# Gate logits of six row blocks from three bf16 parts, put two units later

## The chip, the cores and the metric

One core of a Trainium2 chip runs the whole program. The metric is the device time of one execution in microseconds. Five engines work on it side by side, each with its own queue in program order: TensorE (PE, with its weight loads PEld), VectorE (DVE), ScalarE (ACT), GpSimd (POOL) and SyncE (SP), which issues most DMAs. POOL issues the indirect DMAs, the gathers and scatters by row numbers.

## What is computed

Attention in chunks, then two mixture-of-experts layers, all in float32. The second layer chooses one expert for a token from the first layer's output, so the first layer's rows have to be multiplied by the second layer's gate weights:

```python
def _moe_ref(x, w_gate, w_noise, noise, w1, w2):        # layer one, 1536 rows of 512, 8 experts
    noisy = x @ w_gate + np.log1p(np.exp(x @ w_noise)) * noise
    top2, top2_w = ...                                   # two experts for a row, with weights
    out[mask] += top2_w[mask, k, None] * (np.maximum(x[mask] @ w1[e], 0) @ w2[e])

def _moe2_ref(x, w_gate, w1, w2, capacity):              # layer two
    logits = x @ w_gate                                  # the gate logits
    expert_idx = np.argmax(logits, axis=1)
    ...
```

## The kernel before

Attention runs first (0 to about 75 us). Then come jobs, one for an expert and its rows, in the order `V0, V8, S0 to S6` (layer one) and `U0, UL, R0 to R6` (layer two). A job gathers its rows (POOL), turns them on PE (`x_block`) while the job before still runs, and works in **units**: in an M job (up to 384 rows) eight units of `layer1`, then two units of `rows` for each block of 128 rows. A W job (more rows, or V8) makes its second product in turned form. Products are made in three passes of fp32r parts (`mm3`), for which ACT rounds each raw weight tile (`whi`, L792) and DVE takes the rest (`wlo`, L793).

The finished rows of a block are scattered and added into the DRAM tensor `x_rows`, with the eight gate logits of layer two behind each row. Blocks of V0 and of the M jobs S4, S5 and S6 (ten in all) get their logits in two steps, which stand in the list `todo` and are taken one in a unit, after the unit's matmuls: `row_columns` turns the rows on PE and ACT copies them to `yt` (L1021, L1022); `row_logits` multiplies them by `wg2` in fp32 (L1028), DVE copies the eight columns behind the row (L1029), and POOL scatters (L1035), with a small memset ahead. The second step is called put here. Before, it followed one unit after the first.

After the matmuls of a unit comes what `due` gives: the turning of the next job's rows, hooks, and the splits of weight tiles. So a unit's ACT queue holds, in this order, the eviction of the unit, the copy to `yt`, the next job's `xh`, and `whi`.

During V8 the routing of layer one still runs on DVE between the units (one-hot products, L443 to L483). At the end of S4 `overflow_done` calls `rest1`, a loop for rows over an expert's place, which stands in a branch that is not taken with these inputs; every engine reads the count, passes the branch (L1273) and raises its semaphore behind it. In S6 the list of U0's rows is made from the logits of all jobs up to S5 (`early`), and U0's gather and first turning follow in S6's last units.

Of the kernel before, what the change touches and what calls it, by code (L numbers as in the profile page):

```python
# [8 lines left out]
F32 = mybir.dt.float32  # L9
F32R = mybir.dt.float32r  # L10
F16 = mybir.dt.float16
BF = mybir.dt.bfloat16
I32 = mybir.dt.int32
AF = mybir.ActivationFunctionType
OP = mybir.AluOpType
AX = mybir.AxisListType
# [42 lines left out]
def attention_two_moe_kernel(  # L59
# [7 lines left out]
    nc = tc.nc  # L67
    B, H, S, D = q.shape
    NM = mem_k.shape[2]
    DM, E = w_gate1.shape  # L70
    FF = w1a.shape[2]
# [5 lines left out]
    KD = DM // 128  # L77
# [5 lines left out]
    W2 = DM + 8  # L83
# [8 lines left out]
    pools = {}  # L92

    def pool(name, side="left", **kw):
        st_ = ExitStack()
        pools[name] = st_
        return st_.enter_context(tc.tile_pool(name=name, bufs=1, side=side, **kw))

    consts = pool("consts")
# [8 lines left out]
    def bank(tag):  # L108
        return ps["p"].tile([128, 512], F32, name="ps" + tag, bufs=2)
# [85 lines left out]
    xb, st = {}, {}  # L195
    lgs = axp.tile([128, NT, 2 * V], F32, name="lgs")
    noi = axp.tile([128, NT, V], F32, name="noi")
    wg1 = consts.tile([128, KD, 2 * V], F32, name="wg1")
    wg2 = consts.tile([128, KD, E], F32, name="wg2")

    def xs(t):
        if t not in xb:
            xb[t] = axp.tile([128, DM], F32, name="xs", bufs=4)
        return xb[t]
# [11 lines left out]
    act_copy = lambda d, s: nc.scalar.activation(d, s, AF.Copy)  # L216
# [180 lines left out]
    def y_consts():  # L397

        for i in range(2):
            nc.vector.tensor_copy(yid[:, :, i, 0:128], ident[:, None, :].to_broadcast([128, KD, 128]))  # L400
            nc.vector.tensor_copy(yid[:, :, i, 128:136], wg2)
        nc.vector.tensor_tensor(yid[:, :, 0, 136:144], wg2, yid[:, :, 0, 128:136], op=OP.subtract)
        nc.vector.tensor_copy(yid[:, :, 1, 136:144], zero[:, 0:32].rearrange("p (k e) -> p k e", k=KD))

    def all_of(gen):

# [394 lines left out]
    def x_block(xg, blk, C, tag="B", later=False):  # L801
        n = min(128, C - 128 * blk)
        p = bank(tag)
        pv = p.rearrange("p (k n) -> p k n", k=KD)
        for c in range(KD):
            nc.tensor.transpose(pv[:, c, 0:128], xg[:, c * 128:(c + 1) * 128], ident)  # L806
        o = slice(128 * blk, 128 * blk + n)
        xh, xl = st["x"]
        nc.scalar.activation(xh[:, :, o], pv[:, :, 0:n], AF.Copy)  # L809
        low = lambda: nc.vector.tensor_tensor(xl[:, :, o], pv[:, :, 0:n], xh[:, :, o], op=OP.subtract)  # L810
        if not later:
            low()
        return low
# [199 lines left out]
        nc.scalar.activation(yr[:n, 0:DM], ps[:n], AF.Copy, scale=g[:n])  # L1013
        return yr

    def row_columns(yr, n):

        p = bank("B")
        pv = p.rearrange("p (k n) -> p k n", k=KD)
        for k in range(KD):  # L1020
            nc.tensor.transpose(pv[:, k, 0:n], yr[:n, 128 * k:128 * k + 128], ident[:n, :n])  # L1021
        nc.scalar.activation(st["yt"][:, :, 0:n], pv[:, :, 0:n], AF.Copy)  # L1022

    def row_logits(yr, n):

        p = bank("D")
        for k in range(KD):
            nc.tensor.matmul(p[:n, 0:E], st["yt"][:, k, 0:n], wg2[:, k], start=k == 0, stop=k == KD - 1)  # L1028
        nc.vector.tensor_copy(yr[:n, DM:W2], p[:n, 0:E])  # L1029
# [56 lines left out]
    class Job:  # L1086


        def __init__(self, kind, n0, C, first, ids=None, gate=None, cols=None):
            self.kind, self.n0, self.C, self.first = kind, n0, C, first  # L1090
            self.nb = -(-C // 128)
            self.ids, self.gate, self.cols, self.oids = ids, gate, cols, None
            self.W = W1 if first else W2
            self.whole = C == 64 or cols == 0
            self.late = None
            self.turns = {"W": [8, 10, 12, 14], "M": [8, 9, 10, 11], "T": TT}[kind]
            self.xg = None
            self.later = []
            self.pops = 4 if kind == "T" else 1
            self.quiet = 0 if kind == "T" else 1  # L1100
            self.pool = ()
            self.weigh = 1 if kind == "T" else 5
            self.prev = []
            self.g = []

        def fetch(self):
# [28 lines left out]
        def rows(self, blk, half_, between=None):  # L1135
            if self.cols == 0:
                rows0(half_, between)
            else:
                rows2(self.n0, blk, half_, self.C, between)
            if half_ == 0:  # L1140
                return
            n = min(128, self.C - 128 * blk)
            yr = weighted(st["l2"], self.g[blk], n)
            if self.first:
                def put():
                    row_logits(yr, n)
                    scatter(yr, n, self.ids[blk], True, self.prev)
                self.todo += [lambda: row_columns(yr, n), put]
                return
            f = lambda: scatter(yr, n, (self.oids or self.ids)[blk], False, self.prev)  # L1150
            if self.oids is None:
                self.later.append(f)
            else:
                f()
# [113 lines left out]
    def rest1(wa, wb, ov, en, nb, after):  # L1268

        fl, idf, nvi = ov  # L1270
        n = nc.values_load(nvi[0:1, 0:1], min_val=0, max_val=V * nb)
        b_ = wp["C"]
        with tc.If(n > 0):  # L1273
            with tc.For_i(0, n):
                se, _, idi = picked(b_, fl, idf, nb)
                r = expert_of(b_, se, en)
                xg = b_.tile([128, 4, 256], F32, name="oraw", bufs=1).rearrange("p k f -> p (k f)")
                gather(x_d, idi[:, 0:1], xg[:, 0:W1])
                x_block(xg, 0, 128)
                g = wp["A"].tile([128, 1], F32, name="gs", bufs=10)  # L1280
                gate1(xg, se, g)
                hi, lo = st["y"]

                def part(src):

                    raw = b_.tile([128, 4, 256], F32, name="oraw", bufs=1)
                    nc.sync.dma_start(raw, src)
                    nc.scalar.activation(hi[:, :, 0:256], raw, AF.Copy)
                    nc.vector.tensor_tensor(lo[:, :, 0:256], raw, hi[:, :, 0:256], op=OP.subtract)
                    return [(hi[:, k, 0:256], lo[:, k, 0:256]) for k in range(4)]  # L1290

                xh, xl = st["x"]
                for f in range(4):
                    ws = part(wa[ds(r, 1)].rearrange("e (k p) f -> p (e k) f", p=128)[:, :, 256 * f:256 * f + 256])
                    ps = bank("A")
                    mm3(ps[:, 0:256], [((xh[:, k, 0:128], xl[:, k, 0:128]), ws[k]) for k in range(KD)])
                    nc.scalar.activation(st["hr"][:, 256 * f:256 * f + 256], ps[:, 0:256], AF.Relu)
                for c in range(2):
                    turn(c, 128)
                hh, hl = st["h"]  # L1300
                ps = bank("C")
                for c in range(2):
                    for j in range(2):
                        ws = part(wb[ds(r, 1)].rearrange("e (k p) f -> p (e k) f", p=128)
                                  [:, 4 * j:4 * j + 4, 256 * c:256 * c + 256])
                        mm3(ps[:, 256 * c:256 * c + 256],
                            [((hh[:, 4 * j + k, 0:128], hl[:, 4 * j + k, 0:128]), ws[k]) for k in range(4)],
                            j == 0, j == 1)
                yr = weighted(ps, g, 128)
                row_columns(yr, 128)  # L1310
                row_logits(yr, 128)
                scatter(yr, 128, idi[:, 0:1], True, [])
            after()
# [122 lines left out]
    V0 = Job("T", 0, caps1[0], True, cols=0)  # L1436
# [4 lines left out]
    n = 0  # L1441
# [86 lines left out]
    wp["B"] = pool("wpB")  # L1528
    st["h"] = (wp["B"].tile([128, FB, CM], F32R, name="hh"), wp["B"].tile([128, FB, CM], F32R, name="hl"))
    st["hr"] = wp["B"].tile([128, FF], F32, name="hr")  # L1530
    st["yt"] = wp["B"].tile([128, KD, 128], F32, name="yt")
    st["hf"] = st["yt"].rearrange("p k (j n) -> p (k j) n", n=64)
    st["h0"] = wp["B"].tile([128, 4, 128], F32, name="h0"), st["yt"]
# [5 lines left out]
    S = [Job(kind1(caps1[1 + s]), 4 + 4 * s, caps1[1 + s], True) for s in range(E - 1)]  # L1539
# [80 lines left out]
    def drain():  # L1620
        if bg["gen"] is not None:
            all_of(bg["gen"])
            bg["gen"] = None
# [174 lines left out]
    def overflow_done():  # L1798

        drain()  # L1800

        rest1(w1a, w2a, ov[1], en1, NB1, lambda: x_block(S[5].xg[0], 0, S[5].C))

    hooks = {}
    bg["gen"], bg["next"] = chain(), bg["credit"]
# [37 lines left out]
    U0.late = drain  # L1843
    U0.weigh = UWE
    U0.pool = (1, 3)
    S[0].quiet = S[-1].quiet = U0.quiet = 0
    U0.turns = [2 * U0.nb + 6.5]
    S[-1].turns = [11, 12, 13]
# [10 lines left out]
    for job in jobs[1:-1]:  # L1859
        n = job.n0  # L1860
# [71 lines left out]
```

## Time and profile before

| | |
|---|---|
| time, median of 3 runs | 598.99 us (598.37 to 599.94) |
| the profiled execution | 599.92 us, span 598.1 us |
| PE busy | 582.7 us (97%), 4536 matmul passes |
| DVE, ACT, POOL busy | 62%, 51%, 28% |
| granted clock of PE | 0.999 of full speed |
| `wg2` product (L1028) | 80 passes, 10 blocks |

The page gives the busy time of each engine; the timeline gives single instructions with start and duration, and in brackets the idle time before them with what ended it. Passes of PE overlap, so what a group costs is read from start to start.

### The profile page before, as it was taken

The numbers are of one execution on the slowest core, as the hardware profiler recorded it, in microseconds if no ns is written. First come the engines' busy times: TensorE is split into PE (matmuls) and PEld (weight loads), VectorE is DVE, ScalarE is ACT, GpSimd is POOL, SyncE is SP. The second block draws the span as 40 slices with busy tenths as digits, with TensorE's granted clock in tenths as the row PEclk, the third lists the DMA queues.
The fourth block names the chain that finished last, engine by engine and source line by source line (L and its number), as shares of the span: only waits on it lengthen the run. The fifth ranks groups of instructions, "written<-read, shape, count | busy, mean of one in ns | idle before, by whom it ended". The sixth has DMA issues, their size and how long they took to land. (4 is left out here: it accounts for less than half of the span.)

```text
span 598.1 us, 12264 instructions
## 1 busy us (share of the span) xinstructions
PE 582.7 (97%) x4536; PEld 519.6 (87%) x4548; DVE 369.9 (62%) x984; ACT 303.7 (51%) x638; POOL 166.6 (28%) x242
## 2 busy tenths in 40 slices
PE   8999999999999999999999999999999999999996
PEld 5798756899999999999998898988978978879984
DVE  7888766977555556555555257273668648457672
ACT  5764543455445445445455345344427657466562
POOL 8896104135213114113130321202341121220110
PEclk9999999999999999999999999999999999999999
DMA  9996747475856757647455674654376586975750
GB/s 265 278 214 169 232 128 231 125 228 158 278 159 129 232 159 188 187 130 175 142 110 160 141 157 137 121 140 130 40 248 221 172 267 214 393 270 179 245 188 25
DMA packets 75293, 110.13 MB, mean 184 GB/s; under 512 B 28083, under 2 KB 28083, under 8 KB 75226
## 3 DMA queue, kind: packets, MB, share of 16 engines
q1 hardware_dynamic: 65866, 84.72, 45.5%
q0 software_dynamic: 9360, 24.54, 17.9%
q8 instruction: 38, 0.62, 0.4%
q14 instruction: 29, 0.24, 0.1%
HBM read 88.63 MB, written 20.48 MB: 182 GB/s over the span
## 5 line engine op out<-in xcount | busy, mean ns | idle before, releaser
L793 DVE TENSOR_TENSOR wlo<-raww,whi 128x512 fp32r<-128x512 f32 x226 | 150.4, 689 | 40.1 <-ACT whi L792 38.7
L792 ACT ACTIVATE whi<-raww 128x512 fp32r<-128x512 f32 x228 | 135.6, 624 | 4.3 <-PE psA L858 1.7
L870 DVE SCALAR_TENSOR_TENSOR hl<-psA,hh 128x256 fp32r<-128x256 f32 (+7 forms) x104 | 53.4, 513 | 74.7 <-ACT hh L869 71.0
L869 ACT ACTIVATE hh<-psA 128x256 fp32r<-128x256 f32 (+7 forms) x104 | 47.3, 455 | 99.0 <-PE psA L858 91.6
L858 PE MATMUL psA<-xh,wlo 128*128 128x256 f32 (+7 forms) x416 | 84.8, 325 | 1.5 <-issue 0.7
L858 PE MATMUL psA<-xl,whi 128*128 128x256 f32 (+7 forms) x416 | 82.3, 320 | 0.0
L858 PE MATMUL psA<-xh,whi 128*128 128x256 f32 (+7 forms) x416 | 82.1, 319 | 0.0
L1035 POOL DMA_INDIRECT x_rows<-yr,ids x25 | 39.2, 1570 | 124.3 <-ACT whi L792 82.0
L858 PEld LDWEIGHTS psA<-xh,wlo 128*128 128x128 f32 x416 | 66.4, 188 | 3.8 <-issue 1.2
L858 PEld LDWEIGHTS psA<-xl,whi 128*128 128x128 f32 x416 | 68.1, 188 | 0.7 <-DVEq L1273 0.2
L858 PEld LDWEIGHTS psA<-xh,whi 128*128 128x128 f32 x416 | 68.2, 188 | 0.3
L798 POOL DMA_INDIRECT xg<-x_rows,ids x37 | 37.8, 1022 | 109.9 <-DVE gs L1075 40.8
L858 PE MATMUL psC<-wlo,hh 128*128 128x512 f32 (+1 forms) x184 | 52.7, 406 | 0.0
L858 PE MATMUL psC<-whi,hh 128*128 128x512 f32 (+1 forms) x184 | 51.1, 396 | 0.0
L858 PE MATMUL psC<-whi,hl 128*128 128x512 f32 (+1 forms) x184 | 50.1, 394 | 0.0
L810 DVE TENSOR_TENSOR xl<-psB,xh 128x512 fp32r<-128x512 f32 (+4 forms) x32 | 20.4, 639 | 36.7 <-ACT xh L809 34.7
L858 PEld LDWEIGHTS psC<-whi,hl 128*128 128x128 f32 (+1 forms) x184 | 34.1, 186 | 8.2
L858 PEld LDWEIGHTS psC<-whi,hh 128*128 128x128 f32 (+1 forms) x184 | 33.9, 186 | 8.2
L858 PE MATMUL psA<-hh,wlo 128*128 128x312 f32 (+4 forms) x160 | 36.8, 351 | 0.8 <-DVE hl L870 0.5
L809 ACT ACTIVATE xh<-psB 128x512 fp32r<-128x512 f32 (+4 forms) x32 | 17.7, 555 | 38.8 <-PE psB L806 36.2
L858 PEld LDWEIGHTS psC<-wlo,hh 128*128 128x128 f32 (+1 forms) x184 | 32.1, 186 | 5.6
L1013 ACT ACTIVATE yr<-psC,gs 128x512 f32<-128x512 f32 (+1 forms) x24 | 16.5, 687 | 39.2 <-PE psC L858 34.9
(368 smaller groups left out, 922.2 us busy)
## 6 DMA issues: line engine op xcount, KB each, us to landing
raww<-in_moe_w_dram SPq DMA_DIRECT2D x114, 512.0 KB
raw<-in_k_dram SPq DMA_DIRECT2D x6, 512.0 KB
raw<-in_q_dram SPq DMA_DIRECT2D x6, 512.0 KB
x_rows<-xs SPq DMA_DIRECT2D x12, 256.0 KB
out_dram<-zero SPq DMA_DIRECT2D x3, 1024.0 KB
x_rows<-zero POOLq DMA_DIRECT2D x5, 520.0 KB
v<-in_v_dram SPq DMA_DIRECT2D x10, 256.0 KB
whi<-in_moe_w_dram SPq DMA_DIRECT2D x4, 512.0 KB
```

Source lines behind the costliest of these rows:

```text
L792: nc.scalar.activation(hi[:, c], raw, AF.Copy)
L793: (eng or nc.vector).tensor_tensor(lo[:, c], raw, hi[:, c], op=OP.subtract)
L798: return nc.gpsimd.indirect_dma_start(out=xg, out_offset=None, in_=src, in_offset=bass.IndirectOffsetOnAxis(ap=ids_ap, axis=0))
L809: nc.scalar.activation(xh[:, :, o], pv[:, :, 0:n], AF.Copy)
L810: low = lambda: nc.vector.tensor_tensor(xl[:, :, o], pv[:, :, 0:n], xh[:, :, o], op=OP.subtract)
L858: nc.tensor.matmul(ps, w[a], x[b], start=first and i == 0, stop=last and i == n - 1)
L869: nc.scalar.activation(hh[:, f, 0:C], ps[:, 0:C], AF.Relu)
L870: nc.vector.scalar_tensor_tensor(hl[:, f, 0:C], ps[:, 0:C], 0.0, hh[:, f, 0:C], op0=OP.max, op1=OP.subtract)
L1013: nc.scalar.activation(yr[:n, 0:DM], ps[:n], AF.Copy, scale=g[:n])
L1035: wr = nc.gpsimd.indirect_dma_start(out=x2_d, out_offset=off, in_=yr[:n], in_offset=None, compute_op=OP.add)
```

## The change

The gate weights `wg2` are split once, on POOL, into three bf16 parts (`wg3`, 24 columns). For one block of V0, two of S4, two of S5 and one of S6 the turned rows `yt` are split into three bf16 parts `y3`, in the memory of `hr`: first part by ACT, difference by POOL, second part by ACT, third part by POOL. Their logits are twelve bf16 matmuls of 24 columns instead of four fp32 matmuls of eight, and DVE adds the three groups of eight while it copies them out. The put of such a block now comes two units after the turning: if the job's next block is turned then, right before that, in the same step; otherwise behind two empty steps. The overflow loop gets its own tile for `hr`.

```diff
+    wg3 = consts.tile([128, KD, 3 * E], BF, name="wg3")
+    wgr = consts.tile([128, KD, E], F32, name="wgr")
...
+        three(nc.gpsimd.tensor_copy, [wg3[:, :, E * i:E * i + E] for i in range(3)], wg2, wgr)
+
+    def three(put, b, x, r):
+
+        put(b[0], x)
+        nc.gpsimd.tensor_tensor(r, x, b[0], op=OP.subtract)
+        put(b[1], r)
+        nc.gpsimd.tensor_tensor(b[2], r, b[1], op=OP.subtract)
...
-    def row_columns(yr, n):
+    def row_columns(yr, n, parts=False):
...
+        if parts:
+            three(act_copy, st["y3"], st["yt"], st["h0"][0])
-    def row_logits(yr, n):
+    def row_logits(yr, n, parts=False):
         p = bank("D")
+        if parts:
+            for k in range(KD):
+                for i in range(3):
+                    nc.tensor.matmul(p[:n, 0:3 * E], st["y3"][i][:, k, 0:n], wg3[:, k],
+                                     start=k + i == 0, stop=k == KD - 1 and i == 2)
+            nc.vector.tensor_reduce(yr[:n, DM:W2], p[:n, 0:3 * E].rearrange("p (s e) -> p e s", s=3),
+                                    axis=AX.X, op=OP.add)
+            return
...
             if self.first:
+                parts = n == 128 and blk < self.parts
                 def put():
-                    row_logits(yr, n)
+                    row_logits(yr, n, parts)
                     scatter(yr, n, self.ids[blk], True, self.prev)
-                self.todo += [lambda: row_columns(yr, n), put]
+                before, self.put = self.put, put
+
+                def columns():
+                    if before is not None:
+                        before()
+                    row_columns(yr, n, parts)
+                self.todo.append(columns)
+                if blk == self.nb - 1 or blk >= self.parts:
+                    self.todo += [lambda: None] * (2 if parts else 0) + [put]
+                    self.put = None
                 return
...
+    st["y3"] = [st["hr"].bitcast(BF)[:, 512 * i:512 * i + 512].rearrange("p (k n) -> p k n", k=KD) for i in range(3)]
...
+        op = pool("op", "right")
+        hr, st["hr"] = st["hr"], op.tile([128, FF], F32, name="ohr")
         rest1(w1a, w2a, ov[1], en1, NB1, lambda: x_block(S[5].xg[0], 0, S[5].C))
+        st["hr"] = hr
+        pools["op"].close()
...
+    for job, m in ((V0, 1), (S[4], 2), (S[5], 2), (S[6], 1)):
+        job.parts = m
```

## Rows read from the trace of the kernel before

**Rows 1.** The page, part 1: busy us (share of the span) xinstructions.
```profile
PE 582.7 (97%) x4536; PEld 519.6 (87%) x4548; DVE 369.9 (62%) x984; ACT 303.7 (51%) x638; POOL 166.6 (28%) x242
```

**Rows 2.** Timeline of PE in S5: start us, us, engine, line, operation, count.
```profile
369.18 1.09 PE L858 MATMUL psC<-whi,hl 128*128 128x512 f32 x4
370.11 0.95 PE L1028 MATMUL psD<-wg,yt 128*128 128x8 f32 x8
370.92 1.21 PE L858 MATMUL psC<-wlo,hh 128*128 128x512 f32 x4
```

**Rows 3.** Timeline of PE in U0's stage.
```profile
436.41 1.17 PE L858 MATMUL psC<-whi,hl 128*128 128x512 f32 x4
437.43 0.47 PE L496 MATMUL psD<-oh_Rl,oh_Ll 128*128 128x27 f16 x12
437.74 0.94 PE L858 MATMUL psC<-wlo,hh 128*128 128x512 f32 x3
```

**Rows 4.** Timeline of ACT in V8's stage.
```profile
103.95 0.60 ACT L1022 ACTIVATE yt<-psB 128x512 f32<-128x512 f32 x1
104.45 0.62 ACT L792 ACTIVATE whi<-whi 128x512 fp32r<-128x512 f32 x1
```

**Rows 5.** V8's stage: DVE's busy time in a window, timelines of DVE and PE.
```profile
104.00:118.50 14.50, 13.75 (x33) 1.00 0.51 144
...
105.10 0.69 DVE L793 TENSOR_TENSOR wlo<-whi 128x512 fp32r<-128x512 f32 x1
106.06 0.48 DVE L870 SCALAR_TENSOR_TENSOR hl<-psA,hh 128x312 fp32r<-128x312 f32 x1 [0.27 <-ACT hh L869]
...
116.45 0.84 PE L858 MATMUL psA<-hh,wlo 128*128 128x312 f32 x4 [0.50 <-DVE hl L870]
```

**Rows 6.** POOL by line (busy us, mean ns | idle); timelines of POOL and DVE.
```profile
L1035 POOL DMA_INDIRECT x_rows<-yr,ids x25 | 39.2, 1570 | 124.3 <-ACT whi L792 82.0 <-DVE wlo L793 18.1 <-issue 5.7
...
L793 POOL TENSOR_TENSOR wlo<-raww,whi 128x512 fp32r<-128x512 f32 x2 | 2.6, 1292 | 2.5 <-ACT whi L792 2.5
...
51.84 2.64 POOL L140 COPY v<-v 32x520 f32<-32x520 f32 x4
...
53.21 0.64 DVE L564 TENSOR_TENSOR nz<-nz,lgs 128x32 f32<-128x32 f32 x1
...
81.44 0.23 DVE L564 TENSOR_TENSOR nz<-nz,lgs 128x64 f32<-128x64 f32 x1
```

**Rows 7.** PE's waits at L858 (us, times); DVE's instruction at L1273 (first, last start).
```profile
  DVEq L1273: 0.2, 1
  ACTq L1273: 0.2, 1
...
L1273 DVEq EVENT_SEMAPHORE  x1: 21/21/21, 339.5 to 339.5; - x1
```

**Rows 8.** Timeline of PE in S4 and S5: the turning of later blocks.
```profile
334.42 0.60 PE L1021 MATMUL psB<-ident,yr 128*128 128x128 f32 x4
...
373.82 0.60 PE L1021 MATMUL psB<-ident,yr 128*128 128x128 f32 x4
...
380.02 0.60 PE L1021 MATMUL psB<-ident,yr 128*128 128x128 f32 x4
```

**Rows 9.** Timelines of DVE, POOL and ACT at the end of S4.
```profile
331.70 0.17 DVE L1029 COPY yr<-psD 128x8 f32<-128x8 f32 x1 [1.32 <-PE psD L1028]
...
332.60 1.76 POOL L1035 DMA_INDIRECT x_rows<-yr,ids  x1 [17.37 <-ACT whi L792]
...
335.12 0.60 ACT L1022 ACTIVATE yt<-psB 128x512 f32<-128x512 f32 x1 [2.43 <-PE psB L1021]
...
337.83 0.69 ACT L1013 ACTIVATE yr<-psC,gs 128x512 f32<-128x512 f32 x1 [1.59 <-PE psC L858]
```

**Rows 10.** Timelines of POOL and PE in S6: U0's gather and its turning.
```profile
405.18 1.02 POOL L798 DMA_INDIRECT xg<-x_rows,ids_u  x1 [18.96 <-DVE ids_u L1701]
...
410.04 0.66 PE L806 MATMUL psB<-ident,xg 128*128 128x128 f32 x4 [0.57 <-DMA xg<-x_rows,ids_u]
```

More of the change, by code (lines that the diff above doesn't have):

```diff
@@ L1103, in __init__ @@
             self.prev = []
+            self.parts = 0
+            self.put = None
             self.g = []
@@ L1144, in rows @@
             if self.first:
+                parts = n == 128 and blk < self.parts
                 def put():
-                    row_logits(yr, n)
+                    row_logits(yr, n, parts)
                     scatter(yr, n, self.ids[blk], True, self.prev)
-                self.todo += [lambda: row_columns(yr, n), put]
+                before, self.put = self.put, put
[6 more added lines that the diff above has]
+                    self.todo += [lambda: None] * (2 if parts else 0) + [put]
+                    self.put = None
                 return
```

## The prediction

> **What bounds the kernel now.** I read the page first: TensorE (PE) is busy for 97% of the span [rows 1], so a change pays only if it shortens PE's own line of work, and costs wherever it makes PE wait. Next I read how long a block's gate logits hold that line [rows 2], and what a run of short 16-bit matmuls costs in the same place [rows 3]. Then, since the new work lies on ScalarE (ACT) and GpSimd (POOL), the timelines of the stages where the six blocks stand: the first job of layer one (V8's stage, 104 to 119 us), the end of S4 (327 to 340), the end of S5 (373 to 380) and the end of S6 (405 to 410). In each I asked which engine ends the next wait of PE.
>
> In V8's stage it is not PE. VectorE (DVE) is busy for 13.75 of 14.50 us [rows 5], and PE waits for its `hl` [rows 5]. At the end of S4 every engine passes the branch of `rest1` (L1273); behind it PE's first matmul waits for ACT's event and its fifth for DVE's, 0.2 us each [rows 7]. At 410.04 PE waits 0.57 us for U0's gathered rows [rows 10]. From S4 to S6 there is otherwise no idle time of PE worth a row.
>
> **PE's part of the change.** The eight passes of the fp32 product hold PE from 370.11 to 370.92, 0.81 us, where a group of four matmuls takes 0.93 [rows 2]. Twelve f16 matmuls of 27 columns with twelve different weights hold it for 0.31 us [rows 3]; the new twelve (bf16, 24 columns) are of that form, so I take 0.31. That saves 0.50 a block, 3.0 us for six, if PE is the bound in every place. The reduction that replaces the copy on DVE reads 24 columns instead of eight; the copy takes 0.17 [rows 9], and three times that size on DVE cannot cost more than 0.1 more (an estimate). It sits in PE's shadow and counts as nothing; if that is gone it costs 0.6 in all.
>
> **The path of the three parts.** After the transposes ACT makes `yt` as before, then b0 (ACT), the rest r (POOL), b1 (ACT), the second rest b2 (POOL). An ACT copy of 128x512 takes 0.62 us and starts 0.50 after the one before it [rows 4]. A POOL subtraction of that size takes 1.29 us [rows 6]; there is no row with a bf16 operand, so this is the nearest, and the bounds are a one-input POOL copy of 520 columns (2.64/4 = 0.66 [rows 6]) and twice 1.29. I allow 0.07 us for each hand-over (an estimate). b1 stands in ACT's queue: from the end of b0 to the end of b1 (1.29 + 0.62 + 0.14 = 2.05 us) ACT does nothing for anyone. Behind it wait the weight splits `whi`, with them DVE's `wlo`, and the evictions `hh` and `yr`. That is the cost; "two units later" protects only PE's read of b2.
>
> *V0's block (in V8's stage).* Before, `whi` follows `yt` at 104.45 and `wlo` starts at 105.10 [rows 4, 5]. Now b0 takes that place and ends at 105.07, POOL is free and does r until 106.43, b1 ends at 107.12, `whi` at 107.64. Meanwhile b2 runs on POOL from 107.19 to 108.48. DVE operations with two SBUF inputs stretch beside a POOL operation that reads SBUF: the small L564 took 0.64 us beside the `v` copies, and with twice the elements 0.23 alone [rows 6]. `wlo` is such an operation, so I start it at 108.5, not 107.7: 3.4 (or 2.6) us late. DVE has 0.27 us of idle time before the next `hl` [rows 5], and the copy that moves away gives 0.1 back: 3.0 us remain (2.2 without the blocking). DVE works without a break until 119 and PE already waits for it, 0.50 us at 116.45 [rows 5], so they go through to PE one for one, and the 0.50 saved is swallowed there. **+3.0.**
>
> The Trainium skill ("SBUF — State Buffer", Who interferes with whom) states this as a rule: a DVE instruction with two SBUF inputs and a GpSimd instruction that reads SBUF exclude each other, and the one that issues second waits to the end. The stretched L564 agrees. By the rule the wait is the whole of b2, as taken; were it not so, V8's loss would be 2.2 and the sum 3.75.
>
> *S4's two blocks.* Block 0: r, b1, b2 fit into the two units; b2 ends by 332.2, PE reads it from 333.6. Block 1: the transposes move from 334.42 to 333.92 [rows 8] (0.81 out, 0.31 in), `yt` follows 0.70 later as now [rows 8, 9], b0 ends at 335.74. But POOL must first scatter block 0, whose put has moved right before: reduction until 334.3, then 0.73 us to the scatter's start as now (331.70 + 0.17 to 332.60 [rows 9]), 1.57 us of scatter [rows 6]: r runs from 336.6 to 337.9, b1 to 338.6, then `whi` and the `yr` that now stands at 337.83 [rows 9]. ACT reaches the branch at about 339.75 and DVE, whose `wlo` stands behind `whi` and b2, at 340.75; now DVE's event is at 339.5 and PE's fifth matmul goes right behind it [rows 7]. It comes 1.25 us later in spite of both savings. Put 1, now behind the branch, costs 0.31 and a transition of 0.1 (the group behind an insertion takes 1.02, not 0.93 [rows 2, 3]). **+1.65.**
>
> *S5's two blocks.* The same order without the branch. From 373.82 [rows 8] less 0.50: r waits for the scatter until 376.0, b1 ends at 378.0, b2 at 379.36. PE is at put 1 at 378.71 (380.02 [rows 8] less 1.62 plus 0.31) and its third matmul needs b2: 0.65 us of waiting. 1.0 saved, 0.65 lost: **-0.35** (from -1.0 to +0.6 with POOL's bounds).
>
> *S6's block.* Its put leaves the unit before U0's transposes. But those wait for the gather issued at 405.18 [rows 10], and the program order that leads to it lies before the put; PE only comes earlier and waits 1.4 us instead of 0.57. Then 0.31 and 0.1 follow behind the wait. **+0.4.**
>
> *The rest.* Four small POOL operations on the gate weights in the attention stage, each below the 0.66 of a POOL copy [rows 6]; behind them stands a memset that is not urgent: 0, from 0 to 0.5. POOL's scatters start up to 4 us later and nobody waits for them before the list that follows S5, whose last scatter keeps its place. The extra tile for the overflow loop has no instruction outside that branch: 0.
>
> **Sum.** 3.0 + 1.65 - 0.35 + 0.4 = +4.7 us. The profiled execution took 599.92 us (span 598.1), 0.9 above the median of three, 598.99; it would come to 604.6, and I predict the median: **603.7 us**.
>
> **Rivals.** (1) *Hidden after all:* ACT's hold does not reach PE. Then V8 gives 0 (the saved 0.50 falls into the wait at 116.45), S4 and S5 -1.0 each, S6 +0.4: -1.6, 597.4 us, not slower. It decides where ACT loses less than the 0.75 us that DVE has idle in V8's stage [rows 5] and nothing before the branch. For it: ACT has gaps of 1.6 and 2.4 us in S4 [rows 9]. Against: one POOL step alone is 1.29. 12%. (2) *V8 loses, the branch does not:* if what PE waits for behind the branch is its own event and not ACT's and DVE's, S4 keeps its 1.0, and S5, if its scatter holds POOL no longer than the issue, too: 3.0 - 1.0 - 1.0 + 0.4 = +1.4, 600.4 us. For it: the two waits are short now; against: they are named for both engines [rows 7]. 14%. (3) *POOL is slower with a bf16 operand:* at 1.9 us a step, two steps lie on each of the three long paths, 3 x 1.2 more: 607.3 us, and 611 at the bound of 2.58. 8%. (4) *POOL is quicker:* at 0.66 a step V8 +1.7, the branch +0.3, S5 -1.0, S6 +0.4: 600.4 us. 4%. The forecast, with 601.8 to 605.8 of its own, has 62%.
>
> **How the numbers follow.** A measurement of this kernel tells 0.3% (1.8 us) from no change, so slower begins at 600.8. Slower: the forecast, (3), and half of (2): 77%. Within: most of (1), half of (2), most of (4): 20%. Faster: 3%. The range leaves out (1) and (3) and takes in the rest: 600.1 to 606.4.
>
> **What would show it.** The twelve matmuls of a block at about 0.3 us; ACT idle for 1.3 us or more between b0 and b1, released by POOL; DVE idle for 2.5 us or more near 105 us and PE's waits in V8's stage grown by about 3 us in all; in S4 r behind the scatter and PE's wait at the branch grown from 0.2 to over 2 us; in S5 a wait of 0.65 before the third of the twelve; U0's wait at 1.4. I am wrong if ACT runs other work between b0 and b1, if V8's stage is no longer than before, or if PE's first matmul of S5 waits for ACT no longer than now.

## The result and the profile after

The changed kernel takes 602.96 us (median of six executions, 601.96 to 603.33) and the kernel before, run beside it, 598.98. The ratio is 1.0056, with a 95% interval from 1.0040 to 1.0071: 2.4 to 4.2 us slower. I had predicted 603.7 us with a range from 600.1 to 606.4. The profiled execution took 602.97 us, its span is 601.1.

The page's first line after the change (busy time, share of the span, instructions), and PE's waits (engine, tile and line, released by what: us in total, times, longest):

```profile
PE 582.2 (97%) x4572; PEld 517.3 (86%) x4572; DVE 371.4 (62%) x984; ACT 309.7 (52%) x650; POOL 180.8 (30%) x258
...
PE psA L868 <- DVE hl L880: 3.7, 4, 1.6
PE psA L868 <- ACTq L1306: 2.1, 1, 2.1
...
PE psD L1042 <- POOL spacer L1053: 1.0, 1, 1.0
PE psB L816 <- DMA xg<-x_rows,ids_u: 1.0, 1, 1.0
```

PE is as busy as before, in share [rows 1]. The waits shown, the longest of each kind, stand in the four places of the change: V8's stage, the branch at the end of S4 (L1306, before L1273), the second block of S5, and U0's gathered rows. Before, the branch cost 0.2 us [rows 7] and U0's rows 0.57 [rows 10].

To place the loss I compared when the same matmul groups of PE start in two traces, and took the difference from the begin to the end of a stage. This leaves out the attention stage, whose end differs by up to 3 us between executions of all these kernels. The table has the growth of each stage against the kernel before, in us.

| stage (in the trace of before) | after | kernels of the experiments that change nothing in it |
|---|---|---|
| V8 (95.1 to 136.4) | +2.34 | +0.02 to +0.50 |
| S4 (325.2 to 348.0) | +2.35 | -0.09 |
| S5 (366.1 to 381.2) | +0.09 | +0.04 to +0.07 |
| S6 (402.1 to 419.3) | -0.03 | -0.29 to +0.03, on average -0.17 |

Four timelines of the changed kernel follow (start us, us, engine, line, operation, out<-in, shapes, count, idle time before and its releaser). The first is V8's stage.

```profile
102.56 0.60 ACT L1032 ACTIVATE yt<-psB 128x512 f32<-128x512 f32 x1
103.19 0.63 ACT L218 ACTIVATE hr<-yt 128x512 bf16<-128x512 f32 x1
103.91 1.16 POOL L411 TENSOR_TENSOR h<-yt,hr 128x512 f32<-128x512 f32 x1 [6.34 <-ACT hr L218]
105.10 0.63 ACT L218 ACTIVATE hr<-h 128x512 bf16<-128x512 f32 x1 [1.27 <-POOL h L411]
105.64 0.61 ACT L802 ACTIVATE whi<-whi 128x512 fp32r<-128x512 f32 x1
105.81 1.16 POOL L413 TENSOR_TENSOR hr<-h,hr 128x512 bf16<-128x512 f32 x1 [0.74 <-ACT hr L218]
106.28 1.23 DVE L803 TENSOR_TENSOR wlo<-whi 128x512 fp32r<-128x512 f32 x1 [2.52 <-ACT whi L802]
107.96 0.84 PE L868 MATMUL psA<-xh,wlo 128*128 128x312 f32 x4 [1.60 <-DVE hl L880]
111.65 0.84 PE L868 MATMUL psA<-xh,wlo 128*128 128x312 f32 x4 [1.40 <-DVE hl L880]
```

Between b0 (103.19) and b1 (105.10) ACT runs nothing for 1.27 us, released by POOL. `whi` and `wlo`, which followed `yt` at once [rows 4, 5], come behind that; DVE is idle for 2.52 us, and PE waits 1.60 and 1.40 us for `hl`. The `wlo` at 106.28 takes 1.23 us beside POOL's b2; one alone takes 0.69.

The second timeline is the end of S4 with the branch.

```profile
334.37 0.46 PE L1042 MATMUL psD<-wg,hr 128*128 128x24 bf16 x12
334.69 0.64 PE L1031 MATMUL psB<-ident,yr 128*128 128x128 f32 x4
335.60 1.60 POOL L1055 DMA_INDIRECT x_rows<-yr,ids  x1 [2.53 <-DVE yr L1044]
336.33 0.63 ACT L218 ACTIVATE hr<-yt 128x512 bf16<-128x512 f32 x1
337.11 1.28 POOL L411 TENSOR_TENSOR h<-yt,hr 128x512 f32<-128x512 f32 x1
338.42 0.63 ACT L218 ACTIVATE hr<-h 128x512 bf16<-128x512 f32 x1 [1.47 <-POOL h L411]
338.96 0.61 ACT L802 ACTIVATE whi<-raww 128x512 fp32r<-128x512 f32 x1
339.48 0.67 ACT L1023 ACTIVATE yr<-psC,gs 128x512 f32<-128x512 f32 x1
340.24 0.97 PE L868 MATMUL psA<-xh,wlo 128*128 128x384 f32 x4 [2.14 <-ACTq L1306]
341.97 1.49 PE L868 MATMUL psA<-xh,whi 128*128 128x384 f32 x4
```

The twelve bf16 matmuls hold PE for 0.32 us (334.37 to 334.69). At the branch PE waits 2.14 us for ACT, whose last work ahead of it is the eviction `yr` of the third block. Behind the branch a group of four matmuls takes 1.49 us where it takes 0.86. The granted clock tells why (busy us and count of PE, PEld, DVE, ACT, POOL; then PEclk, DMA share, GB/s):

```profile
341.00:344.50 3.50, 3.50 (x14) 3.50 (x13) 0.44 (x1) 0.49 (x1) 1.54 (x2) 0.57 0.51 161
```

For some three microseconds behind the wait PE runs at its lower level, 1.2 GHz. That is about 1.3 of the 2.35 us of this stage (the same wait with the clock at 1.00 made 1.03, in the run with S4's blocks alone below), and I had not forecast it.

The third is the second block of S5.

```profile
376.18 0.46 PE L1042 MATMUL psD<-wg,hr 128*128 128x24 bf16 x12
376.71 1.29 DVE L803 TENSOR_TENSOR wlo<-raww,whi 128x512 fp32r<-128x512 f32 x2
377.91 0.18 DVE L1044 TENSOR_REDUCE yr<-psD 128x8 f32<-128x24 f32 x1
378.37 1.57 POOL L1055 DMA_INDIRECT x_rows<-yr,ids  x1 [3.52 <-DVE yr L1044]
379.40 1.73 POOL L411 TENSOR_TENSOR h<-yt,hr 128x512 f32<-128x512 f32 x1
381.17 0.63 ACT L218 ACTIVATE hr<-h 128x512 bf16<-128x512 f32 x1 [2.68 <-POOL h L411]
381.88 1.15 POOL L413 TENSOR_TENSOR hr<-h,hr 128x512 bf16<-128x512 f32 x1 [0.74 <-ACT hr L218]
383.09 0.41 PE L1042 MATMUL psD<-wg,hr 128*128 128x24 bf16 x10 [1.02 <-POOL spacer L1053]
```

The first block's product is done at 376.5, but its reduction waits on DVE behind two `wlo` until 377.91, the scatter waits for the reduction, and r waits on POOL for the scatter: b0 ends at 378.49, and r, whose record begins before the scatter's ends, is done at 381.13, 2.76 us behind the scatter's start (2.79 in S4). PE begins the second block's product, and its third matmul waits 1.02 us; b2 ends at 383.03, so the releaser is b2 (the spacer's tiny memset is merely POOL's last instruction by then).

### The profile page after: what moved, and what is told of

The parts are those of the page before. It is cut to its first block, busy times and chain, and to the rows that moved or that the text cites. A ratio compares the mean times of both kernels' runs of the same rounds, so it can differ in the third digit from the quotient of the medians.

```text
span 601.1 us, 12351 instructions
## 1 busy us (share of the span) xinstructions
PE 582.2 (97%) x4572; PEld 517.3 (86%) x4572; DVE 371.4 (62%) x984; ACT 309.7 (52%) x650; POOL 180.8 (30%) x258
## 5 line engine op out<-in xcount | busy, mean ns | idle before, releaser
L868 PE MATMUL psA<-xh,wlo 128*128 128x256 f32 (+7 forms) x416 | 85.6, 327 | 6.4 <-DVE hl L880 3.2
L868 PE MATMUL psA<-xh,whi 128*128 128x256 f32 (+7 forms) x416 | 82.8, 321 | 0.0
L868 PE MATMUL psA<-xl,whi 128*128 128x256 f32 (+7 forms) x416 | 82.7, 321 | 0.0
L868 PEld LDWEIGHTS psA<-xh,wlo 128*128 128x128 f32 x416 | 67.1, 190 | 9.3 <-DVE hl L880 4.3
L868 PEld LDWEIGHTS psA<-xl,whi 128*128 128x128 f32 x416 | 68.5, 189 | 0.7 <-DVE xl L820 0.3
L868 PEld LDWEIGHTS psA<-xh,whi 128*128 128x128 f32 x416 | 68.8, 189 | 0.3
L868 PE MATMUL psC<-wlo,hh 128*128 128x512 f32 (+1 forms) x184 | 52.4, 404 | 0.0
L868 PE MATMUL psC<-whi,hh 128*128 128x512 f32 (+1 forms) x184 | 51.0, 396 | 0.0
L868 PE MATMUL psC<-whi,hl 128*128 128x512 f32 (+1 forms) x184 | 50.1, 394 | 0.0
L868 PEld LDWEIGHTS psC<-whi,hl 128*128 128x128 f32 (+1 forms) x184 | 34.1, 186 | 8.1
L868 PEld LDWEIGHTS psC<-whi,hh 128*128 128x128 f32 (+1 forms) x184 | 33.8, 186 | 8.1
L1062 POOL DMA_INDIRECT out_dram<-yr,oids x12 | 12.0, 997 | 86.8 <-ACT yr L1023 54.1
L868 PE MATMUL psA<-hh,wlo 128*128 128x312 f32 (+4 forms) x160 | 36.9, 351 | 0.8 <-DVE hl L880 0.5
L868 PEld LDWEIGHTS psC<-wlo,hh 128*128 128x128 f32 (+1 forms) x184 | 32.2, 186 | 5.8
```

The costliest lines, as they stand in the source:

```text
L868: nc.tensor.matmul(ps, w[a], x[b], start=first and i == 0, stop=last and i == n - 1)
L1062: wr = nc.gpsimd.indirect_dma_start(out=out, out_offset=off, in_=yr[:n, 0:DM], in_offset=None, bounds_check=N - 1, oob_is_err=False)
```

## The experiments

Theory: making the parts costs what it holds up on other engines, in V8's stage and at the branch; PE's savings reach the end only in S4 and S5, where a wait eats them. The rivals: the loss is an accident of two profiles; the moved puts are the cost; POOL's reading beside DVE is the cost; the clock is the cost. Ratios stand against the kernel before, run in the same series.

**V0's block alone.**

```diff
-    for job, m in ((V0, 1), (S[4], 2), (S[5], 2), (S[6], 1)):
+    for job, m in ((V0, 1),):
```

> Only V0's block is made from three parts; S4, S5 and S6 keep the fp32 product. Theory: its price is paid where it stands and mostly stays. In the trace of the changed kernel V8's stage is 2.6 us longer (PE waits 1.60 and 1.40 us for hl), and 0.45 us of that is taken back before S4 (a wait for gathered rows and one more that PE meets later): +2.2 us against the kernel before, about 601.2 if that stands at 599.0. Rival: the stage's delay is an accident of this pair of profiles, whose attention stages already end 1.45 us apart, or is taken back wholly by later waits: 0, within 0.5 us of the kernel before.

Measured: ratio 1.0030 (1.0011 to 1.0050), that is 0.7 to 3.0 us slower. V8's stage grew by 2.22 us and the other three by -0.09, +0.04 and -0.15. PE's two waits for `hl` are those of the changed kernel, to 0.01 us:

```profile
110.24 0.84 PE L868 MATMUL psA<-xh,wlo 128*128 128x312 f32 x4 [1.61 <-DVE hl L880]
...
113.92 0.84 PE L868 MATMUL psA<-xh,wlo 128*128 128x312 f32 x4 [1.41 <-DVE hl L880]
```

The rival that takes it for an accident falls; the loss stays to the end. Kernels that leave this stage alone show up to 0.50 (on average 0.27), so some 2.0 us are V0's.

**S4's blocks alone.**

```diff
+    for job, m in ((S[4], 2),):
```

> Only S4's two blocks are made from three parts. Theory: +2.4 us against the kernel before, the sum of 1.0 saved by the two shorter products (0.5 each), 2.1 of waiting of PE at the branch, and 1.4 in the first units of S5, whose matmuls run at a granted clock of 0.50 for some 3 us behind that wait; the span then shows the wait at L1306 near 2 us and a stretch at 0.50. Rival 1: without V0's block ACT and DVE come to the branch as early as before, PE waits less than 0.5 us, and the two blocks save 1.0 us: -1.0. Rival 2: the wait comes but the clock stays: +1.0 to +1.65, as I forecast.

Measured: ratio 1.0023 (1.0004 to 1.0043), 0.2 to 2.6 us slower; S4's stage grew by 1.03 us. The branch waits as long as in the changed kernel, but the clock stays (first PE at the branch, then the clock behind it):

```profile
339.91 0.97 PE L868 MATMUL psA<-xh,wlo 128*128 128x384 f32 x4 [2.14 <-ACTq L1306]
```

```profile
341.00:344.00 3.00, 3.00 (x19) 3.00 (x18) 0.56 (x1) 0.49 (x1) 1.38 (x2) 1.00 0.49 175
```

So the second rival holds, my forecast as it stood before the result: the wait without the clock. The same wait of 2.14 us went with a fallen clock in one execution and not in another, and S4's own price is about 1.1 us, not 2.4.

**S5's and S6's blocks alone.**

```diff
+    for job, m in ((S[5], 2), (S[6], 1)):
```

> Only the two blocks of S5 and the one of S6 are made from three parts. Theory: about +0.1 us against the kernel before: S5 saves 1.0 and PE then waits about 1.0 for the last part of its second block (I forecast 0.65), S6's gain falls into U0's wait for gathered rows and its put adds 0.3 behind it: 0 to +0.4 in all. Rival: the wait in S5 is a consequence of the shift that S4 had made (its scatter lies closer to the copies); without it POOL is earlier, PE does not wait, and the run is 0.6 to 1.0 us faster than the kernel before.

Measured: ratio 1.0008 (0.9990 to 1.0026). S5's stage grew by 0.15, with the same wait (1.04 us) before the third of the twelve; it is not a consequence of S4. S6's grew by 0.49: U0's rows are waited for 1.47 us. In the changed kernel that wait is 1.02 and the stage is no longer than before, so S6's price, beyond the -0.17 of kernels that leave the stage alone, lies between 0.1 and 0.7 us, by when the rows land.

**S4's blocks with PE kept busy at the branch.**

```diff
         drain()
+        warm(6)
...
+    for job, m in ((S[4], 2),):
```

> S4's two blocks alone from three parts, as in the run before the last, and six idle bf16 matmuls of 512 columns on PE right before the branch, so that PE stands still for about 1.3 us less there and nobody else does anything more. Theory: the matmuls of S5's first units are slow because the granted clock falls to 0.50 behind PE's 2.1 us of idleness; with it filled the clock stays at 1.00 and the run is 1.2 to 1.4 us faster than the one with S4's blocks alone, about +1.0 against the kernel before. Rival: S5's first units are held by something else (their weights, DVE), the clock being a companion: the time is that of S4's blocks alone, within 0.4 us, or the six matmuls cost up to 1.3 us more.

Measured: ratio 1.0019 (1.0001 to 1.0037); S4's stage grew by 1.03, as without the six matmuls. The wait shrinks to 0.83 us and PE goes on at the same moment:

```profile
338.52 1.47 PE L254 MATMUL psD<-warmer 128*128 128x512 bf16 x6
340.82 0.97 PE L868 MATMUL psA<-xh,wlo 128*128 128x384 f32 x4 [0.83 <-ACTq L1306]
```

Since the clock had not fallen in the run to compare with either, this doesn't test the clock. It shows that PE's time ahead of the branch is free there.

**PE's part without the parts.**

```diff
-        nc.scalar.activation(st["yt"][:, :, 0:n], pv[:, :, 0:n], AF.Copy)
-        if parts:
-            three(act_copy, st["y3"], st["yt"], st["h0"][0])
+        nc.scalar.activation((st["y3"][0] if parts else st["yt"])[:, :, 0:n], pv[:, :, 0:n], AF.Copy)
...
-                    nc.tensor.matmul(p[:n, 0:3 * E], st["y3"][i][:, k, 0:n], wg3[:, k],
+                    nc.tensor.matmul(p[:n, 0:3 * E], st["y3"][0][:, k, 0:n], wg3[:, k],
```

> All six blocks, with the twelve bf16 matmuls and the later puts, but without the work that makes the parts: the copy of the turned rows is written as bf16 once and stands for all three parts, so neither ACT nor POOL does anything more than before (the second and third part are left out of the computation). Theory: this is PE's part of the change alone. V0's 0.5 falls into PE's wait in V8's stage, S4 and S5 give 1.0 each, S6's falls into U0's wait: -1.5 to -2.0 us against the kernel before, and about 6 us below the changed kernel (4.0 above). So all that the changed kernel loses, and these 2 us more, is the price of making the parts. Rival: the later puts themselves cost (put 1 of S4 behind the branch, S6's behind U0's wait): no gain, within 0.7 us of the kernel before. Second rival: every one of the six saves its 0.5: -3.0.

Measured: ratio 1.1969, some 118 us slower, and no answer to the question. Its psC groups of L868 count 208 matmuls each, against 184: blocks were worked through that the kernel otherwise skips, I take it because other logits choose other experts and more rows overflow. A part that decides what work is done can't be left out to measure its price; the last experiment asks the same from the other side.

**V0's block with all four steps on POOL.**

```diff
-            three(act_copy, st["y3"], st["yt"], st["h0"][0])
+            three(nc.gpsimd.tensor_copy, st["y3"], st["yt"], st["h0"][0])
...
+    for job, m in ((V0, 1),):
```

> Only V0's block is made from three parts, and all four steps of its parts are done by POOL, so that ACT is never held between two of its copies. Theory: V8's stage loses because ACT stands still for some 1.3 us and does 1.26 us of copies, and the weight splits behind them come late; DVE's stretched wlo (1.23 for 0.69 us) adds only 0.5. Then this run loses at most 0.5 to 1.0 us, against 2.2 with ACT's copies. Rival: what costs is POOL's reading of SBUF beside DVE (about 4 us of it now, over five or six of DVE's operations): the run loses as much as with ACT's copies or more, +2 to +3 us.

Measured: ratio 1.0019 (1.0010 to 1.0028), 0.6 to 1.7 us slower. V8's stage grew by 0.50, the upper end of what kernels show that leave it alone. Last comes PE's one new wait in the stage.

```profile
103.31 0.60 ACT L1032 ACTIVATE yt<-psB 128x512 f32<-128x512 f32 x1
103.81 0.62 ACT L802 ACTIVATE whi<-whi 128x512 fp32r<-128x512 f32 x1
103.98 0.62 POOL L410 CAST hr<-yt 128x512 bf16<-128x512 f32 x1 [5.70 <-ACT yt L1032]
104.46 0.69 DVE L803 TENSOR_TENSOR wlo<-whi 128x512 fp32r<-128x512 f32 x1
105.95 0.78 DVE L803 TENSOR_TENSOR wlo<-whi 128x512 fp32r<-128x512 f32 x1
107.80 0.69 DVE L463 TENSOR_SCALAR oh_hi<-oh_pi 128x16 int32<-128x16 int32 x1
110.62 0.84 PE L868 MATMUL psA<-xh,wlo 128*128 128x312 f32 x4 [1.49 <-DVE hl L880]
```

`whi` follows `yt` at once and `wlo` follows that, as in the kernel before. DVE's operations beside POOL are stretched (0.78 for 0.69; 0.69 for 0.17 in L463), and PE waits 1.49 us for `hl` at 110.62, where the kernel before hardly waits (with ACT's copies it was 1.61 and 1.41). So the rival has a part in it: up to there the stage is 0.82 us longer, with PE's shorter product already in it, and 0.3 of that is gone again at its end. With ACT's copies it is 2.53 up to there and 2.22 at the end. In the traces, then, ACT's two copies and its standing still between them make up some 1.7 of V0's 2.2 us. By the times alone the two runs can't be told apart: their intervals overlap.

**S4's and S5's blocks with the subtractions on DVE.**

```diff
-        nc.gpsimd.tensor_tensor(r, x, b[0], op=OP.subtract)
+        eng.tensor_tensor(r, x, b[0], op=OP.subtract)
...
-            three(act_copy, st["y3"], st["yt"], st["h0"][0])
+            three(act_copy, st["y3"], st["yt"], st["h0"][0], nc.vector)
...
+    for job, m in ((S[4], 2), (S[5], 2)):
```

> Only S4's and S5's blocks from three parts, and their two subtractions are done by DVE (0.69 us each, and idle there) and not by POOL (1.16 to 1.73 us, and behind a scatter). Theory: the price in S4 and S5 is the time of POOL's steps and of the scatter ahead of them. With DVE ACT stands still for about 0.8 us and not 1.4, comes to the branch with DVE no later than in the kernel before, and the last part is there before PE wants it: the four blocks keep 0.4 to 0.5 each, -1.6 to -2.0 us against the kernel before, faster than both kernels. Rival: ACT's two further copies (1.26 us a block) are enough to make PE wait at the branch and for the first evictions of S5: between 0 and +1.5.

Measured: ratio 0.9988 (0.9979 to 0.9998), 0.1 to 1.3 us faster. S5 gave 1.08 us, all that PE saves there; its wait is gone. S4 gave nothing (+0.09), for PE still waits at the branch:

```profile
337.54 0.61 ACT L802 ACTIVATE whi<-raww 128x512 fp32r<-128x512 f32 x1
338.06 0.67 ACT L1023 ACTIVATE yr<-psC,gs 128x512 f32<-128x512 f32 x1
338.83 0.97 PE L868 MATMUL psA<-xh,wlo 128*128 128x384 f32 x4 [1.43 <-ACTq L1306]
```

**One block of S4 and one of S5, made by ACT and POOL.**

```diff
+    for job, m in ((S[4], 1), (S[5], 1)):
```

> Only the first block of S4 and the first of S5 from three parts, as the changed kernel makes them (ACT and POOL). Theory: the first blocks are hidden; what costs is the second block of each, whose rest waits behind the first block's scatter and which stands next to the branch in S4. This run keeps 0.5 us for each: -1.0 us against the kernel before, and PE's wait at the branch stays near 0.2. Rival: already the first block delays ACT's and DVE's weight splits so that they come late to the branch: 0 to +1.0.

Measured: ratio 0.9988 (0.9976 to 0.9999). S4 gave 0.52 (0.43 beyond kernels that leave the stage alone), S5 0.56, as expected; PE's wait at the branch is 0.36 us. The first blocks are hidden, and what costs is the second.

**The blocks that showed no wait, together.**

```diff
+            self.parts = ()
...
+                parts = n == 128 and blk in self.parts
...
+                if blk == self.nb - 1 or blk not in self.parts:
...
+    for job, m in ((S[4], (0,)), (S[5], (0, 1)), (S[6], (1,))):
```

with DVE's subtractions as above.

> From three parts, with DVE's subtractions, only the blocks for which the runs so far show no wait: the first of S4, the first two of S5, and the second of S6, which stands behind U0's wait for gathered rows. Theory: S4 gives 0.3 to 0.4 (0.3 in the trace of the run with one block), S5 1.0 (0.98 in the trace of the run with DVE), S6 0.5: -1.7 to -1.9 us against the kernel before. Rival: S6's put, held to the columns of its third block, and ACT's two copies delay U0's weights: S6 gives nothing or takes 0.5, -0.8 to -1.3.

Measured: ratio 0.9993 (0.9978 to 1.0008). S4 gave 0.29 and S5 1.09, but S6's stage grew by 0.44: the rival. Its held put meets DVE and ACT, and PE waits where it had not before.

```profile
416.49 0.41 PE L1042 MATMUL psD<-wg,hr 128*128 128x24 bf16 x10 [0.26 <-DVE hr L413]
417.34 0.66 PE L1031 MATMUL psB<-ident,yr 128*128 128x128 f32 x4 [0.44 <-ACT yr L1023]
```

**The third blocks too.**

```diff
+    for job, m in ((S[4], (0, 2)), (S[5], (0, 1, 2)), (S[6], (1, 2))):
```

> As the run before, and also the third blocks of S4, S5 and S6, whose copies fall into the first units of the next job. Theory: ACT and DVE have idle time there (DVE is busy 3.1 us of the 9 from 340 to 349 in the kernel before), so each gives its 0.5 more: -3.0 to -3.4 us. Rival: in these units hh and hl are evicted for every accumulation, and ACT held between its two copies makes PE wait as in V8's stage: the three give nothing or cost up to 1 us each, -1.8 to +1.

Measured: ratio 1.0073 (1.0054 to 1.0092), 4.4 us slower by the medians, beyond both expectations. The price stands in two places. At the list behind S5, PE falls 2.6 us further behind the kernel before in a single wait:

```profile
400.01 0.18 PE L1728 MATMUL psD<-em,tri 128*128 128x12 bf16 x1 [2.42 <-DVE em L1724]
```

```profile
397.62 0.25 DVE L433 TENSOR_REDUCE fm_m<-lg 128x12 f32<-128x96 f32 x1 [3.40 <-DMA lg<-x_rows]
```

The list behind S5 reads all logits back (`lg`), S5's last put stands two units later, and DVE waits 3.40 us for that transfer; PE waits 2.42 us for `em`. The prediction had leaned on this put keeping its place in the change. The other place is S6's third block, where PE loses some 3 us more: its product begins before the parts are made, and the clock is at 0.52 from 426 to 429.

```profile
425.11 0.19 PE L1042 MATMUL psD<-wg,hr 128*128 128x24 bf16 x1 [1.20 <-ACT hr L218]
```

So the rival's hold of ACT is at most a part of it, and the late put, which neither expectation had, is nearly as dear.

**The put of S4's second block alone, moved behind the branch.**

```diff
-                self.todo += [lambda: row_columns(yr, n), put]
+                if self is S[4] and blk == 1:
+                    self.put = put
+                    self.todo.append(lambda: row_columns(yr, n))
+                elif self is S[4] and blk == 2:
+                    self.todo += [lambda: (self.put(), row_columns(yr, n)), put]
+                else:
+                    self.todo += [lambda: row_columns(yr, n), put]
```

> The kernel before, with no parts anywhere; only the put of S4's second block (its fp32 product of eight passes, copy and scatter) is moved from ahead of the branch to the columns of the third block, where the changed kernel has it. Theory: PE's wait at the branch is for ACT's eviction of the third block's rows, which begins when PE's last matmul ends, so it is about 1.4 us long whatever PE does meanwhile; the product ahead of it was free. The wait grows from 0.2 to 1.2 or 1.4, and the run is 0.9 to 1.0 us slower than the kernel before. Rival: the put costs the same on either side of the branch: within 0.3 us.

Measured: ratio 1.0019 (1.0005 to 1.0032), 0.3 to 1.9 us slower; S4's stage grew by 0.59. The direction is the theory's. The medians differ by 0.96, the size that the theory has, but in the trace the size lies between the two: PE's wait is 0.82 us, not 1.2 to 1.4, as `yr` has no `whi` ahead of it here.

```profile
338.34 0.96 PE L858 MATMUL psA<-xh,wlo 128*128 128x384 f32 x4 [0.82 <-ACTq L1279]
```

**The making of the parts alone.**

```diff
-                    row_logits(yr, n, parts)
+                    row_logits(yr, n)
...
+                self.todo += [lambda: row_columns(yr, n, parts), put]
```

> The kernel before on PE (fp32 products of eight passes, puts where they were), with the making of the parts added for all six blocks on ACT and POOL as in the changed kernel; nobody reads the parts (the shorter products are left out). It is the price of the parts alone. Theory: V8's stage +2.2 as with V0's block alone; at the branch of S4 ACT comes 0.7 to 0.9 later; S5 and S6 have no reader to wait: +2.9 to +3.4 us against the kernel before, so that PE's part of the change, shorter products and moved puts together, gives nothing in the changed kernel (4.0 above). Rival: the parts cost about 6 and PE's part gives its 2 us back.

Measured: ratio 1.0069 (1.0048 to 1.0091), 2.9 to 5.5 us slower. By stages: V8 +2.76, S4 +2.43, S5 +0.04, S6 -0.21. In both of the first two the clock fell behind PE's wait:

```profile
115.00:118.00 3.00, 3.00 (x13) 3.00 (x13) 2.40 (x5) 1.30 (x3) 0.00 (x0) 0.50 0.04 8
...
343.00:346.00 3.00, 2.38 (x7) 2.38 (x8) 1.28 (x2) 0.52 (x1) 2.12 (x3) 0.61 0.20 64
```

The clock has its share in this price. One of the six executions had a granted clock of 0.999 and took 602.79 us, 2.8 above the median of the kernel before; the others, at 0.990 to 0.995, took 603.5 to 606.3. The changed kernel's six lie at 0.995 to 0.998.

The price of the parts alone is that of the whole change, within the intervals: by the medians PE's part, shorter products and moved puts together, returns some 0.5 us, which can't be told from nothing, nor from the difference in clock. The rival's price of 6 lies outside the interval.

## Why the prediction was right, point by point

- **PE's part.** Right: 0.31 forecast for twelve matmuls, 0.32 measured. That all six blocks save 0.50 only if PE is the bound was the proper doubt: S5 with DVE gives 1.08 for two blocks, V8 and S6 none.
- **The path of the parts.** Right in its form. From the end of b0 to the end of b1 I had 2.05 us; it is 1.91 in V8's stage, since a subtraction takes 1.16 us there and not 1.29. It rises to 1.28 in S4, and to 1.73 for the one in S5 whose record overlaps a scatter. Rival 3 (POOL slower with a bf16 operand) falls, and so does 4.
- **V8, +3.0.** The mechanism is shown by V0's block alone and by V0 on POOL. The mis-sized term is its amount: 2.64 us where the job's second product begins (117.64 for 116.45, from a stage that began 1.45 earlier), of which 0.30 was gone again at the stage's end: 2.34, and about 2.1 beyond what other kernels show on average. "One for one" held inside the stage and not to its end. DVE's `wlo` did not stand still until b2 was over, as I had put it; it began at 106.28 and ended at 107.51, 0.54 behind b2's end. The Trainium skill ("SBUF — State Buffer", Who interferes with whom) would have it wait to b2's end and then run; the record shows one longer span, 1.23, that ends 0.15 earlier than that would. The rule agrees in direction and nearly in amount.
- **S4, +1.65.** About 1.1 us where the clock stays, and 2.35 in the profiled execution, where it falls. The sign is right, and the engine that decides was the wrong one of two. I had DVE's event decide, by way of PE's fifth matmul; in the trace PE waits once, for ACT, and the fifth matmul follows 0.81 behind the first without a wait. I had misread [rows 7]: its two waits are those of PE's weight loads, and the fifth matmul of the kernel before does not stand still for the second.

```profile
339.55 0.65 PEld L858 LDWEIGHTS psA<-xl,whi 128*128 128x128 f32 x4 [0.21 <-DVEq L1273]
339.56 0.97 PE L858 MATMUL psA<-xl,whi 128*128 128x384 f32 x4
```

The wait for ACT can be taken apart by runs: 0.21 at the weight load (0.15 at the matmul) with the product ahead of the branch, 0.82 with the put moved behind it, 1.43 with ACT's copies and DVE's subtractions, 2.14 with POOL's. "r behind the scatter" is there but small in S4: b0 ends at 336.96, r starts at 337.11; I had 0.9 us.
- **S5, -0.35.** +0.1: the wait before the third matmul is 1.02 us where I had 0.65. The step that failed is the reduction "in PE's shadow": it stood on DVE behind two `wlo` (377.91, its product done at 376.5), held the scatter, and the scatter r. The run with DVE's subtractions takes POOL out of the path, and the wait is gone.
- **S6, +0.4.** Right within what the rows' landing makes of it: 0.1 in the changed kernel, 0.7 alone. U0's wait of 1.4 was 1.02 and 1.47.
- **The sum.** V8 was 0.7 to 0.9 too dear and S4 0.55 too dear without the fall of the clock (0.7 too cheap with it); S5 was 0.45 too cheap. By the single runs the four places make 2.0 + 1.1 + 0.1 + 0.1 to 0.7, 3.3 to 3.9 us; measured are 2.4 to 4.2. The median ended 0.7 below the forecast. That it came so near is in part luck: S5's error took back some of V8's and S4's, and the clock, which I had left out, adds to the executions in which it falls. Rival 1 (hidden) falls with V0's block alone; rival 2 (the branch does not lose) falls with S4's alone.
- **Two slips in the working.** Without the blocking of `wlo` the terms give 2.2 + 1.65 - 0.35 + 0.4 = 3.9, not 3.75. S5's upper end with two steps of 2.58 is -0.35 + 2.6, about +2.2, not +0.6; rival 3's 611 has that bound in it. Neither enters the forecast.

A better version is one that leaves V0, S6 and S4's second block as they were. The two runs at 0.9988, which both leave V0 and S6 alone, are faster than the kernel before, though their intervals end close to 1. S4's first block by POOL (-0.52) with S5's two by DVE (-1.08) would be the next to try; that pair was not run.

## What to carry to other kernels

A chain that goes back and forth between two engines costs the first engine the other's time as well, because everything queued behind the second visit waits; look there before you count the work itself. Before a step is moved, ask what it was covering: the fp32 product ahead of the branch filled a wait that PE has anyway, so taking its 0.81 us away saved only about 0.15 there and cost in full behind it. And trace the reader of a moved result to its last consumer, for a list that reads everything back has a due time of its own.

## What was not expected of the hardware

The granted clock fell to its lower level behind a wait of PE in some executions and not in others of the same length: 2.14 us of waiting were followed by 0.57 from 341 to 344.5 us in the changed kernel and by 1.00 with S4's blocks alone; 1.24 us and 1.78 us were followed by 0.61 and 0.50 in the run with the parts alone, while V0's block alone has 1.61 and 1.41 and stays at 1.00 there. In the profiles of five runs, two of those among them, the clock also fell near 82 us, in the attention stage. Of the twelve executions with S4's blocks alone, the two slowest (603.15 and 603.16 us) have the lowest clock over the whole, 0.993; where it fell in them is not on record. What decides it stays open. The cost was about 1.3 us in S4 (2.35 against 1.03); V8's stage with the fall (2.76) is only 0.54 longer than that of V0's block alone, though that kernel also has its put elsewhere. Behind the fall PE no longer has the waits of some 0.5 and 0.3 us for DVE that the other kernels have there.
